# An attention and two-MLP kernel: mask-bit matmuls moved and paired, another order of the first eight periods, other dummy matmuls, a halved last product

## The chip, the core and the metric

The kernel runs on one core of a Trainium2 chip. The metric is the device time of one execution in microseconds (us). The engines are TensorE (PE: matmuls, PEld: the loading of their weights), VectorE (DVE), ScalarE (ACT), GpSimd (POOL) and SyncE (SP, which issues all DMAs here).

## What is computed

Bucketed attention over 2 batches, 8 heads, 768 tokens and 64 dimensions, and behind it two layers on the (2, 768, 512) result: a token-mixing layer with cosines and sines, and a normalized MLP of width 2048. Inputs and output are float32.

```python
q_bits = einsum('bhsd,dk->bhsk', q, proj) > 0        # 6 bits per query, the same for k
mask = q_bucket[:, :, :, None] == k_bucket[:, :, None, :]
scores = where(mask, (q @ k.T) / sqrt(64), -1e9)
attn = exp(scores - max) / (sum + 1e-9)
x = (attn @ v), heads side by side                   # 2 x 768 x 512
theta = x @ w_theta
y = w_tok_r @ (x * cos(theta)) + w_tok_i @ (x * sin(theta))
u = x + y;  x = u + relu(u @ w_ch)
xn = (x - mean) / sqrt(var + 1e-6) * g_ln
out = x + relu(xn @ w_ch1) @ w_ch2
```

## The kernel before

Every factor of a product is split into a high part and a low part of a type that TensorE takes at one pass per column, and a product is the sum of three matmuls (high by high, high by low, low by high). Tile names ending in `hi`/`lo`, `h`/`l` are these parts.

The attention works in 48 *periods* of 256 queries of one head, each with two tiles of 128 queries (i = 0, 1), whose scores stand in the PSUM tiles S0 and S1 (128 x 772 columns used). The steps of a period p have short names, `name.p.i`: the scores' matmuls (`S`, or, for the three periods of the first head, `D` and `Q`), the row maximum on VectorE (`M`, `s_max`, L340), the exponential on ScalarE (`E`, `s_exp`, L356), which is the last reader of S0 or S1, the reciprocal (`R2`), the normalization on GpSimd (`n`), 12 transposes on TensorE into the banks T0, T1, T2 (`U.p.u`), their copies into high and low parts (`H` on ScalarE, `L` on VectorE), 12 matmuls with the values of 256 columns (`PV`, L405) and the evacuation (`O`, `X`).

The mask is made by more rows in the scores' product: the bits of query and key as +-2^34 and the like. For all heads but the first, high, low and bits rows are stacked by DMAs (`sk`, `sb`) into tiles of 128 and 71 rows, and `s_mm` (L332) makes a tile with four matmuls of 386 columns. The first head doesn't wait for that: `direct_mm` (`D.p.i`, L503) makes six matmuls of 386 columns with the parts as they are (64 rows in period 0, 128 rows in periods 1 and 2), opening the accumulation, and `direct_bits` (`Q.p.i`, L515) closes it with two matmuls on the 7 rows of bits.

The bits come from `bits_chunk` (`ac.x` for the first pair of heads, `bc.x` for pairs 1 to 3, L286): two matmuls per pair on 384 columns of the parts, x = 0, 1 the halves of the key, 2, 3 of the query. `ac` writes the banks T0, T1, T2, O; `bc` writes T2 or O. Then ScalarE copies a half (`ay`, `by`), VectorE compares (`ab`, `bb`, L310) and VectorE or GpSimd scales it to the bits rows (`aw`, L523; `bw`, L663). `sh.nm.n.x.e` and `sl.nm.n.x.e` make the high and low part of query or key of pair n (x: half 0 or 1, or 2 for the whole; e: which engine, 0 is ScalarE or VectorE, 1 is GpSimd). `pb` splits the projection, `kz` copies the first head's key parts into tiles whose upper 64 rows are zero, `lr`, `lv` load raw queries, keys and values.

The kernel keeps the order of its instructions on every engine as it is written. For the first eight periods that order is one long list, `head`; each word calls a step. From then on `plan` lists the steps of a period; after the attention `tail`, `half1`, `trans`, `odd`, `even`, `last` are lists in the same manner. `warm(n)` (L493, listed as `warm.17`) puts n transposes of the identity into bank T0; their result is not read. 16 of them are issued right after the first loads, and 17 stand in `head` behind `Q.0.1`.

The end: round 15 of the MLP, `o_mm` (L1180) makes an output tile of 128 x 512 with six matmuls of 512 columns into T0 or O by turns, `o_add` (L1187) adds it to the residue on VectorE and SyncE stores the tile (L1189). Six tiles follow each other there.

Of the kernel before, what the change touches and what calls it, by code (L numbers as in the profile page):

```python
# [33 lines left out]
def attn_moe_kernel(  # L34
# [649 lines left out]
    head = """
        sh.k.0.0.0 pb.0.0 pb.0.2 sl.k.0.0.0 pb.0.1 sh.k.0.1.0 sl.k.0.1.0 sh.q.0.0.0 sl.q.0.0.0 sh.q.0.1.0 ac.0
        sl.q.0.1.0 fk ac.1 ay.0 ay.1 kz.1.1 ac.2 ay.2 D.0.0 ab.0 lr.3.0 ab.1 ac.3 sh.k.1.2.0 D.0.1 ay.3 ab.2
        sh.q.1.2.0 aw.0.1 aw.1.1 pb.1.0 aw.2.0 kz.0.0 ab.3 Q.0.0 M.0.0 Q.0.1 warm.17 pb.1.2 E.0.0 lr.3.1 M.0.1
        sl.q.1.2.1 E.0.1 pb.1.1 D.1.0 sl.k.1.2.0 sh.k.3.2.0 Q.1.0 tb.0 lr.2.0 R2.0 lr.2.1 aw.3.0 M.1.0 n.0.1
        sk.1 sh.k.2.2.0 D.1.1 n.0.0 E.1.0 U.0.2 Q.1.1 U.0.0 sh.q.3.2.0 sl.k.2.2.0 sl.k.3.2.0 U.0.1 sl.q.3.2.1
        H.0.0 D.2.0 M.1.1 H.0.2 bc.0.1 L.0.2 L.0.0 Q.2.0 sh.q.2.2.0 E.1.1 M.2.0 by.0 tb.1 H.0.1 bc.1.0 D.2.1  # L690
        lv.0 bb.0 sl.q.2.2.1 L.0.1 by.1 sb.1 R2.1 Q.2.1 bw.0.1 n.1.0 E.2.0 bb.1 vh.0.0 lr.4.0 bc.3.1 M.2.1
        vh.0.1 S.3.0 lr.5.0 vl.0.0.0 bc.2.0 by.3 bw.1.1 E.2.1 U.1.0 by.2 M.3.0 S.3.1 bb.3 n.1.1 U.1.1 E.3.0
        vl.0.1.1 R2.2 bb.2 U.1.2 tb.2 bw.3.1 H.1.0 M.3.1 n.2.0 H.1.1 S.4.0 PV.0 H.1.2 E.3.1 L.1.0 L.1.1 lr.4.1
        M.4.0 tb.3 R2.3 sh.k.4.0.0 gl U.2.0 n.2.1 O.0 n.3.0 bw.2.1 L.1.2 X.0 S.4.1 sl.k.4.0.1 U.2.1 E.4.0 U.2.2
        H.2.0 M.4.1 H.2.1 sk.2 H.2.2 E.4.1 S.5.0 lv.1 sh.q.4.0.0 PV.1 lr.5.1 L.2.0 sb.2 L.2.1 M.5.0 L.2.2 R2.4
        O.1 tb.4 X.1 n.3.1 sh.k.4.1.1 E.5.0 U.3.0 S.5.1 U.3.2 U.3.1 n.4.1 H.3.0 H.3.2 H.3.1 S.6.0 M.5.1 sk.4
        n.4.0 L.3.0 vh.1.0 L.3.2 PV.2 E.5.1 L.3.1 sl.q.4.0.1 U.4.2 O.2 vh.1.1 M.6.0 sk.3 R2.5 X.2 vl.1.0.1
        U.4.0 sb.3 S.6.1 tb.5 H.4.0 sl.k.4.1.0 sb.4 U.4.1 H.4.2 M.6.1 n.5.0 E.6.0 H.4.1 L.4.0 E.6.1 PV.3 n.5.1
        S.7.0 U.5.0 sh.q.4.1.0 O.3 L.4.2 L.4.1 M.7.0 H.5.0 U.5.2 S.7.1 X.3 R2.6 tb.6 U.5.1 E.7.0 H.5.1 H.5.2
        M.7.1 PV.4 vl.1.1.1 L.5.0 sl.q.4.1.1 n.6.0 E.7.1 tb.7 O.4 L.5.1  # L700
    """
# [769 lines left out]
```

## Time and profile before

| | us |
|---|---|
| median of 3 runs | 665.45 (664.65 to 670.51) |
| profiled execution | 665.16 |
| its span, first to last instruction | 663.4 |
| TensorE busy | 657.4 |
| VectorE busy | 556.9 |
| ScalarE busy | 416.7 |
| GpSimd busy | 310.4 |

The profiled execution's time is that of the whole execution; its span runs from its first to its last instruction. Busy shares are averages over stages that differ. In a timeline, instructions of one line that follow each other stand in one row ("x6"): start of the first and time until the end of the last. A matmul's end is modelled: matmuls overlap, so what one costs is read from the distance of their starts, not from its duration. In the chain each piece reaches to the start of the next.

### The profile page before, as it was taken

The numbers are of one execution on the slowest core, as the hardware profiler recorded it, in microseconds if no ns is written. First come the engines' busy times: TensorE is split into PE (matmuls) and PEld (weight loads), VectorE is DVE, ScalarE is ACT, GpSimd is POOL, SyncE is SP. The second block draws the span as 40 slices with busy tenths as digits, with TensorE's granted clock in tenths as the row PEclk, the third lists the DMA queues.
The fourth block names the chain that finished last, engine by engine and source line by source line (L and its number), as shares of the span: only waits on it lengthen the run. The fifth ranks groups of instructions, "written<-read, shape, count | busy, mean of one in ns | idle before, by whom it ended". The sixth has DMA issues, their size and how long they took to land.

```text
span 663.4 us, 11202 instructions
## 1 busy us (share of the span) xinstructions
PE 657.4 (99%) x3769; PEld 591.7 (89%) x3769; DVE 556.9 (84%) x999; ACT 416.7 (63%) x864; POOL 310.4 (47%) x419
## 2 busy tenths in 40 slices
PE   9999999999999999999999999999999999999997
PEld 7999999999999888888888888989998999999996
DVE  6999998999999999999888889986767686867654
ACT  6899998999999886776435534553333433333321
POOL 5887887667787644233433133434150505051400
PEclk9999999999999999999999999999999999999999
DMA  8977544575530411222422122101112121311022
GB/s 247 241 172 171 142 106 114 126 165 124 132 91 1 160 54 57 81 77 98 144 81 64 48 96 68 60 1 64 64 65 75 53 96 34 105 53 33 0 80 111
DMA packets 32230, 62.24 MB, mean 94 GB/s; under 512 B 4466, under 2 KB 11460, under 8 KB 32173
## 3 DMA queue, kind: packets, MB, share of 16 engines
q1 hardware_dynamic: 32173, 61.53, 32.6%
q8 instruction: 30, 0.49, 0.3%
q14 instruction: 27, 0.22, 0.1%
HBM read 39.98 MB, written 3.15 MB: 65 GB/s over the span
## 4 chain that ended last, share of the span: by engine, by line
PE 96%; DVE 2%; DMA 1%; issue 0%; ACT 0%; SPq 0%; POOL 0%; POOLq 0%
PE o L1180 20%; PE acc L853 15%; PE o L405 10%; PE s L332 10%; PE t L380 9%; PE Z L1145 8%; PE a L895 5%; PE v L1145 5%; PE th L787 3%; PE zy L1145 2%; PE Y L1145 2%; PE bits L286 2%; PE s L503 1%; PE warm L493 1%; PE ut L880 1%; PE xt L964 1%
## 5 line engine op out<-in xcount | busy, mean ns | idle before, releaser
L1180 PE MATMUL o<-arena,hh 128*128 128x512 f32 x384 | 118.9, 391 | 0.0
L367 POOL TENSOR_SCALAR pn<-p,l,M 128x768 f32<-128x768 f32 x96 | 94.7, 986 | 38.6 <-DVE l L363 25.8
L340 DVE TENSOR_REDUCE M<-s 128x1 f32<-128x772 f32 x96 | 91.0, 949 | 3.6 <-PE s L515 2.2
L101 DVE TENSOR_TENSOR ptl<-t,pth 128x512 fp32r<-128x512 f32 x144 | 90.6, 680 | 1.5 <-ACT pth L389 1.3
L356 ACT ACTIVATE p<-s,M 128x772 f32<-128x772 f32 x96 | 87.6, 912 | 2.7 <-DVE M L340 2.2
L117 POOL TENSOR_SCALAR cs<-st 128x512 f32<-128x512 f32 (+2 forms) x68 | 44.7, 663 | 84.1 <-DVE cy L131 75.1
L1180 PEld LDWEIGHTS o<-arena,hh 128*128 128x128 f32 x384 | 71.5, 188 | 13.7
L389 ACT ACTIVATE pth<-t 128x512 fp32r<-128x512 f32 x144 | 81.1, 599 | 3.9 <-PE t L380 2.5
L332 PE MATMUL s<-tk,tq 128*128 128x386 f32 (+1 forms) x360 | 82.8, 351 | 0.0
L380 PE MATMUL t<-ident,pn 128*128 128x128 f32 x576 | 80.1, 273 | 0.0
L853 PE MATMUL acc<-arena,tokh 128*128 128x512 f32 x240 | 75.3, 395 | 0.0
L1180 PE MATMUL o<-arena,hl 128*128 128x512 f32 x192 | 75.2, 392 | 0.0
L380 PEld LDWEIGHTS t<-ident,pn 128*128 128x128 f32 x576 | 68.5, 141 | 5.7 <-POOL pn L367 0.6
L1153 ACT ACTIVATE sn<-Z 128x384 f32<-128x384 f32 x39 | 19.2, 492 | 67.2 <-PE Z L1145 67.2
L332 PEld LDWEIGHTS s<-tk,tq 128*128 128x128 f32 (+1 forms) x360 | 59.4, 190 | 0.1
L853 PEld LDWEIGHTS acc<-arena,tokh 128*128 128x128 f32 x240 | 44.0, 188 | 8.5
L1187 DVE TENSOR_TENSOR U<-o,U 128x512 f32<-128x512 f32 x48 | 32.9, 689 | 21.3 <-PE o L1180 20.5
L853 PE MATMUL acc<-arena,tokl 128*128 128x512 f32 x120 | 46.9, 391 | 0.0
L405 PE MATMUL o<-pth,vv 128*128 128x256 f32 x288 | 45.9, 295 | 0.1
L114 ACT ACTIVATE cy<-st 128x512 f32<-128x512 f32 (+2 forms) x72 | 39.6, 562 | 8.1 <-DVE tokl L101 2.5
L131 DVE SCALAR_TENSOR_TENSOR cy<-cy,cs 128x512 uint32<-128x512 uint32 (+2 forms) x72 | 41.4, 575 | 3.6
L125 DVE SCALAR_TENSOR_TENSOR cs<-st,cs 128x512 uint32<-128x512 uint32 (+2 forms) x76 | 44.0, 579 | 0.2
(257 smaller groups left out, 1482.8 us busy)
## 6 DMA issues: line engine op xcount, KB each, us to landing
st<-in_w_dram SPq DMA_DIRECT2D x36, 256.0 KB
st<-in_w_dram SPq DMA_DIRECT2D x14, 512.0 KB
tk<-hik SPq DMA_DIRECT2D x30, 193.0 KB
tq<-hiq SPq DMA_DIRECT2D x30, 192.0 KB
st<-in_wrT_dram SPq DMA_DIRECT2D x12, 384.0 KB
st<-in_wiT_dram SPq DMA_DIRECT2D x12, 384.0 KB
vs<-in_v_dram SPq DMA_DIRECT2D x8, 384.0 KB
tk<-lok SPq DMA_DIRECT2D x15, 193.0 KB
```

The source lines that it names most:

```text
L101: eng.tensor_tensor(out=o, in0=i, in1=f(hi), op=ALU.subtract)
L117: eng.tensor_scalar(out=s, in0=f(t)[:, :, 1], scalar1=0.0, scalar2=1.0, op0=ALU.mult, op1=ALU.mult)
L332: pe.matmul(ps[:, hf, 0:HW], lt[0:K, x * 128:(x + 1) * 128], rt[0:K, hf, :], start=(K == 128), stop=(K != 128),)
L340: vec.tensor_reduce(out=m_t[p][:, 0, i:i + 1], in_=s_ps[p, i][:, :, 0:HW], axis=AX.XY, op=ALU.max, negate=True)
L356: act.activation(pt, ps[:, :, 0:HW], AF.Exp, bias=m[:, 0, i:i + 1], accum_out=l_t[p][:, 0, i:i + 1])
L367: pool.tensor_scalar(out=pn.rearrange("p (h c) s -> p h (c s)", h=2), in0=p_t.pop((p, i))[:, :, 0:HALF], scalar1=l_t[p][:, 1, i:i + 1], sc ...
L380: pe.transpose(ps[:, w * 128:(w + 1) * 128], pn_t[p, i][:, c, :], ident)
L389: act.activation(ph, t_ps[p, u], AF.Copy)
L405: pe.matmul(ps, vv[:, c, e].rearrange("p a d -> p (a d)"), x[:, c::NI, :], start=(k == 0), stop=(k == 2 * NI - 1),)
L853: pe.matmul(acc, w[:, x, t * 128:(t + 1) * 128], z[:, x, y, :], start=(j == 0 and k == 0), stop=(j == NI - 1 and k == 5),)
L1145: pe.matmul(ps_t[r, b], W1[g][y][:, w, d, :], XB[s][x][:, z, d, :], start=(first == 1 and k == 0), stop=(k == 5), skip_group_check=True,)
L1180: pe.matmul(ps, lt[:, i * 128:(i + 1) * 128], W2[g][:, y, x, :], start=(k == 0), stop=(k == 5))
```

## The change

Four things change. `direct_bits` may come before `direct_mm` for a tile of periods 1 and 2: it then makes the tile and opens the accumulation (`start`), and `direct_mm` closes it; the list uses this for i = 1. The list `head` has another order, and other engines for some steps (the last digit of `sh`, `sl`, `aw`, `kz`, `bw`, `vl`), with 19 transposes in place of 17. The first 16 transposes are replaced by 38 matmuls of 128 columns of a tile of zeros by itself, for which VectorE, not GpSimd, clears `pb_lo`, that part first. And the last `o_mm`/`o_add` (tile 5 of the last round) is made in two halves of 256 columns, the first in bank O, the second in S0, each with its own addition and store.

```diff
@@ -494,15 +494,17 @@
 
     def direct_mm(p, i):
 
-        ps = psum.tile([128, 2, 512], F32, tag=f"S{i}", name=f"s{p}_{i}")
-        s_ps[p, i] = ps
+        if (p, i) not in s_ps:
+            s_ps[p, i] = psum.tile([128, 2, 512], F32, tag=f"S{i}", name=f"s{p}_{i}")
+        ps = s_ps[p, i]
+        first, last = (p == 0 or i == 0), (p > 0 and i == 1)
         r = slice((2 * p + i) * 128, (2 * p + i + 1) * 128)
         K, kk = (64, [hl["k", 0, y] for y in (0, 1)]) if p == 0 else (128, kz)
         for x, y in ((0, 0), (0, 1), (1, 0)):
             for hf in range(2):
                 pe.matmul(
                     ps[:, hf, 0:HW], hl["q", 0, x][0:K, r],
-                    kk[y][0:K, hf, :], start=(x + y == 0), stop=False,
+                    kk[y][0:K, hf, :], start=(first and x + y == 0), stop=(last and x == 1),
                 )
 
     def bits_q(r):
@@ -510,11 +512,14 @@
         return bits_t[0][0:7, hf, x:x + 128]
 
     def direct_bits(p, i):
+        lead = (p, i) not in s_ps
+        if lead:
+            s_ps[p, i] = psum.tile([128, 2, 512], F32, tag=f"S{i}", name=f"s{p}_{i}")
         r = slice((2 * p + i) * 128, (2 * p + i + 1) * 128)
         for hf in range(2):
             pe.matmul(
                 s_ps[p, i][:, hf, 0:HW], bits_q(r),
-                bk0[0:7, hf, :], start=False, stop=True,
+                bk0[0:7, hf, :], start=lead, stop=not lead,
             )
 
     def bits_p0(nm, hf, eng):
@@ -542,12 +547,16 @@
     sp.dma_start(out=cst_sb, in_=cst)
     load_raw(1)
     sp.dma_start(out=pbr[:, 1:NP], in_=pb[:, 1:NP])
+    vec.memset(f(pb_lo[:, 1]), 0.0)
+    ps = bank("T0", "warm")[:, 0:128]
+    for x in range(38):
+        pe.matmul(ps, pb_lo[:, 1], pb_lo[:, 1], start=True, stop=True)
+    for n in (0, 2, 3):
+        vec.memset(f(pb_lo[:, n]), 0.0)
     make_identity(nc, ident)
     pool.memset(halfpi, math.pi / 2)
-    pool.memset(f(pb_lo), 0.0)
     for t in kz:
         pool.memset(f(t[64:128]), 0.0)
-    warm(16)
     TS = tuple(range(22, 46, 3))
     bg, bg2, bg3 = {}, {}, {}
 
@@ -682,22 +691,22 @@
     )
 
     head = """
-        sh.k.0.0.0 pb.0.0 pb.0.2 sl.k.0.0.0 pb.0.1 sh.k.0.1.0 sl.k.0.1.0 sh.q.0.0.0 sl.q.0.0.0 sh.q.0.1.0 ac.0
-        sl.q.0.1.0 fk ac.1 ay.0 ay.1 kz.1.1 ac.2 ay.2 D.0.0 ab.0 lr.3.0 ab.1 ac.3 sh.k.1.2.0 D.0.1 ay.3 ab.2
-        sh.q.1.2.0 aw.0.1 aw.1.1 pb.1.0 aw.2.0 kz.0.0 ab.3 Q.0.0 M.0.0 Q.0.1 warm.17 pb.1.2 E.0.0 lr.3.1 M.0.1
-        sl.q.1.2.1 E.0.1 pb.1.1 D.1.0 sl.k.1.2.0 sh.k.3.2.0 Q.1.0 tb.0 lr.2.0 R2.0 lr.2.1 aw.3.0 M.1.0 n.0.1
-        sk.1 sh.k.2.2.0 D.1.1 n.0.0 E.1.0 U.0.2 Q.1.1 U.0.0 sh.q.3.2.0 sl.k.2.2.0 sl.k.3.2.0 U.0.1 sl.q.3.2.1
-        H.0.0 D.2.0 M.1.1 H.0.2 bc.0.1 L.0.2 L.0.0 Q.2.0 sh.q.2.2.0 E.1.1 M.2.0 by.0 tb.1 H.0.1 bc.1.0 D.2.1
-        lv.0 bb.0 sl.q.2.2.1 L.0.1 by.1 sb.1 R2.1 Q.2.1 bw.0.1 n.1.0 E.2.0 bb.1 vh.0.0 lr.4.0 bc.3.1 M.2.1
...
+        sh.k.0.0.0 pb.0.0 sl.k.0.0.0 pb.0.2 pb.0.1 ac.0 sh.k.0.1.0 sl.k.0.1.0 ac.1 sh.q.0.0.0 sh.q.0.1.0
+        sl.q.0.0.0 ay.0 ac.2 sl.q.0.1.0 fk ac.3 ab.0 ay.1 kz.1.1 ay.2 D.0.0 ay.3 lr.3.0 ab.1 D.0.1 ab.2
+        sh.k.1.2.0 lr.2.0 aw.0.1 aw.1.0 aw.2.1 Q.0.0 ab.3 lr.3.1 lr.2.1 pb.1.0 sl.k.1.2.0 pb.1.2 kz.0.1 sk.1
+        sh.q.1.2.0 Q.0.1 warm.19 M.0.0 E.0.0 aw.3.1 sh.k.3.2.1 M.0.1 E.0.1 pb.1.1 sl.k.3.2.0 tb.0 sh.k.2.2.0
+        R2.0 D.1.0 Q.1.1 sl.k.2.2.0 Q.1.0 sh.q.3.2.0 n.0.1 D.1.1 bc.0.1 M.1.0 bc.1.0 n.0.0 M.1.1 U.0.0
+        sh.q.2.2.0 E.1.0 D.2.0 E.1.1 Q.2.1 lv.0 by.1 sl.q.3.2.0 sl.q.1.2.0 Q.2.0 sl.q.2.2.1 bb.1 H.0.0 L.0.0
+        U.0.2 U.0.1 by.0 H.0.2 bb.0 D.2.1 H.0.1 M.2.0 tb.1 bw.0.1 E.2.0 bc.3.1 sb.1 vh.0.0 R2.1 bw.1.0 S.3.0
...
     """
 
     for w in head.split():
@@ -1169,24 +1178,32 @@
         hh, hlo = h_t[r, c]
         vec.scalar_tensor_tensor(out=hlo, in0=c_t.pop((r, c)), scalar=0.0, in1=f(hh), op0=ALU.max, op1=ALU.subtract)
 
-    def o_mm(r, t):
+    def cols(x):
+        return slice(0, 512) if x is None else slice(256 * x, 256 * x + 256)
+
+    def o_mm(r, t, x0=None, tag=None):
         g, s = rounds[r]
         e, i = divmod(t, TB)
-        ps = o_t[r, t] = bank(("T0", "O")[t % 2], f"o{r}{t}")
+        n = cols(x0)
+        if tag == "S0":
+            ps = psum.tile([128, 2, 512], F32, tag=tag, name=f"o{r}{t}")[:, 0, n]
+        else:
+            ps = bank(tag or ("T0", "O")[t % 2], f"o{r}{t}")[:, n]
+        o_t[r, t] = ps
         k = 0
         for x in range(2):
             hh, hlo = h_t[r, 10 * (x + 1) + e + 1]
             for lt, y in ((hh, 0), (hh, 1), (hlo, 0)):
-                pe.matmul(ps, lt[:, i * 128:(i + 1) * 128], W2[g][:, y, x, :], start=(k == 0), stop=(k == 5))
+                pe.matmul(ps, lt[:, i * 128:(i + 1) * 128], W2[g][:, y, x, n], start=(k == 0), stop=(k == 5))
                 k += 1
 
-    def o_add(r, t):
+    def o_add(r, t, x0=None):
         g, s = rounds[r]
         c = ORD[6 * s + t]
-        u = U(c)
+        u = U(c)[:, cols(x0)]
         vec.tensor_tensor(out=u, in0=o_t.pop((r, t)), in1=u, op=ALU.add)
         if g == NG - 1:
-            sp.dma_start(out=out[c * 128:(c + 1) * 128, :], in_=u)
+            sp.dma_start(out=out[c * 128:(c + 1) * 128, cols(x0)], in_=u)
 
 
     ops.update(
@@ -1414,8 +1431,10 @@
         run(last if g == NG else odd if r % 2 else even, r=r, p=r - 1, g=g, a=a, b=b, c=c, d=d)
     r = len(rounds) - 1
     run("o_mm.{r}.0 h_add.{r}.12 h_hi.{r}.12 o_add.{r}.0 h_lo.{r}.12", r=r)
-    for t in range(1, 6):
+    for t in range(1, 5):
         run("o_mm.{r}.{t} o_add.{r}.{t}", r=r, t=t)
+    for x, tag in ((0, "O"), (1, "S0")):
+        run("o_mm.{r}.5.{x}.{tag} o_add.{r}.5.{x}", r=r, x=x, tag=tag)
     order.close()
     zctx.close()
 
```

## Rows read from the trace of the kernel before

**Rows 1.** Page, part 1: busy time (share of the span) and instructions of each engine.

```profile
PE 657.4 (99%) x3769; PEld 591.7 (89%) x3769; DVE 556.9 (84%) x999; ACT 416.7 (63%) x864; POOL 310.4 (47%) x419
```

**Rows 2.** Page, part 4: the chain that ended last, shares by engine.

```profile
PE 96%; DVE 2%; DMA 1%; issue 0%; ACT 0%; SPq 0%; POOL 0%; POOLq 0%
```

**Rows 3.** The chain, first 30 us: start us, us, engine, tile, line, number of instructions.

```profile
1.34 3.69 PE warm L493 x16
...
11.34 2.01 PE warm L493 x17
...
19.32 1.05 PE bits L286 x6
...
25.02 0.71 PE s L332 x4
...
27.94 0.88 PE t L380 x8
...
29.54 1.45 PE o L405 x12
```

**Rows 4.** Timeline, TensorE, 0 to 25 us: start us, us, engine, line, operation, tiles.

```profile
4.59 0.42 PE L493 MATMUL warm<-ident 128*128 128x128 f32 x1
5.07 0.69 PE L286 MATMUL bits<-hik,pb_hi 128*128 128x384 f32 x1
...
5.88 0.52 PE L286 MATMUL bits<-hik,pb_hi 128*128 128x384 f32 x1
...
6.84 0.52 PE L286 MATMUL bits<-loq,pb_lo 128*128 128x384 f32 x1
7.29 0.64 PE L503 MATMUL s<-hik,hiq 64*128 64x386 f32 x2
...
13.14 0.62 PE L503 MATMUL s<-tkz,hiq 128*128 128x386 f32 x2
...
14.39 0.61 PE L515 MATMUL s<-bk,bits 7*128 7x386 f32 x2
...
24.86 0.87 PE L332 MATMUL s<-tk,tq 128*128 128x386 f32 x4
```

**Rows 5.** Timeline, the last matmul and the last addition.

```profile
659.12 0.39 PE L1180 MATMUL o<-arena,hl 128*128 128x512 f32 x1
659.55 0.69 DVE L1187 TENSOR_TENSOR u<-o,u 128x512 f32<-128x512 f32 x1 [0.67 <-PE o L1180]
```

**Rows 6.** Windows: us; busy PE, PEld, DVE, ACT, POOL; granted clock; DMA share; GB/s.

```profile
0.00:5.05 5.05, 3.67 (x16) 3.27 (x16) 0.69 (x2) 2.38 (x5) 2.75 (x12) 1.00 0.52 153
...
660.60:660.90 0.30, 0.00 (x0) 0.00 (x0) 0.00 (x0) 0.00 (x0) 0.00 (x0) 1.00 0.00 0
...
661.50:661.80 0.30, 0.00 (x0) 0.00 (x0) 0.00 (x0) 0.00 (x0) 0.00 (x0) 1.00 0.94 362
```

**Rows 7.** Timeline, VectorE (DVE) and ScalarE (ACT), 3 to 14 us.

```profile
3.66 0.56 DVE L221 SCALAR_TENSOR_TENSOR lok<-raws,hik 128x384 fp32r<-128x384 f32 x1 [3.66 <-ACT hik L210]
...
5.32 0.56 DVE L221 SCALAR_TENSOR_TENSOR lok<-raws,hik 128x384 fp32r<-128x384 f32 x1 [0.97 <-ACT hik L210]
...
5.86 1.05 DVE L101 TENSOR_TENSOR loq<-raws,hiq 128x384 fp32r<-128x384 f32 x2
...
6.86 1.61 DVE L310 SCALAR_TENSOR_TENSOR bb<-bits,by 64x384 f32<-64x384 f32 x3
...
11.03 1.83 DVE L340 TENSOR_REDUCE M<-s 128x1 f32<-128x772 f32 x2 [0.73 <-PE s L515]
...
12.09 0.91 ACT L356 ACTIVATE p<-s,M 128x772 f32<-128x772 f32 x1 [1.14 <-DVE M L340]
...
13.04 0.95 DVE L221 SCALAR_TENSOR_TENSOR lok<-raws,hik 128x768 fp32r<-128x768 f32 x1
```

**Rows 8.** Timeline, GpSimd (POOL), its first operation on a tile.

```profile
0.71 0.20 POOL masks.py:197 MEMSET ident<- 128x128 f32 x1 [0.29 <-POOLq L1461]
```

**Rows 9.** The chain, last 8 us: twenty matmuls of 512 columns.

```profile
654.98 4.55 PE o L1180 x20
```

More of the change, by code (lines that the diff above doesn't have):

```diff
@@ L690, in attn_moe_kernel @@
-        H.0.0 D.2.0 M.1.1 H.0.2 bc.0.1 L.0.2 L.0.0 Q.2.0 sh.q.2.2.0 E.1.1 M.2.0 by.0 tb.1 H.0.1 bc.1.0 D.2.1
-        lv.0 bb.0 sl.q.2.2.1 L.0.1 by.1 sb.1 R2.1 Q.2.1 bw.0.1 n.1.0 E.2.0 bb.1 vh.0.0 lr.4.0 bc.3.1 M.2.1
-        vh.0.1 S.3.0 lr.5.0 vl.0.0.0 bc.2.0 by.3 bw.1.1 E.2.1 U.1.0 by.2 M.3.0 S.3.1 bb.3 n.1.1 U.1.1 E.3.0
-        vl.0.1.1 R2.2 bb.2 U.1.2 tb.2 bw.3.1 H.1.0 M.3.1 n.2.0 H.1.1 S.4.0 PV.0 H.1.2 E.3.1 L.1.0 L.1.1 lr.4.1
-        M.4.0 tb.3 R2.3 sh.k.4.0.0 gl U.2.0 n.2.1 O.0 n.3.0 bw.2.1 L.1.2 X.0 S.4.1 sl.k.4.0.1 U.2.1 E.4.0 U.2.2
@@ L695, in attn_moe_kernel @@
[L695 to L699, printed above, removed]
@@ L700, in attn_moe_kernel @@
-        M.7.1 PV.4 vl.1.1.1 L.5.0 sl.q.4.1.1 n.6.0 E.7.1 tb.7 O.4 L.5.1
+        sh.k.0.0.0 pb.0.0 sl.k.0.0.0 pb.0.2 pb.0.1 ac.0 sh.k.0.1.0 sl.k.0.1.0 ac.1 sh.q.0.0.0 sh.q.0.1.0
+        sl.q.0.0.0 ay.0 ac.2 sl.q.0.1.0 fk ac.3 ab.0 ay.1 kz.1.1 ay.2 D.0.0 ay.3 lr.3.0 ab.1 D.0.1 ab.2
+        sh.k.1.2.0 lr.2.0 aw.0.1 aw.1.0 aw.2.1 Q.0.0 ab.3 lr.3.1 lr.2.1 pb.1.0 sl.k.1.2.0 pb.1.2 kz.0.1 sk.1
+        sh.q.1.2.0 Q.0.1 warm.19 M.0.0 E.0.0 aw.3.1 sh.k.3.2.1 M.0.1 E.0.1 pb.1.1 sl.k.3.2.0 tb.0 sh.k.2.2.0
@@ new lines, in attn_moe_kernel @@
+        R2.0 D.1.0 Q.1.1 sl.k.2.2.0 Q.1.0 sh.q.3.2.0 n.0.1 D.1.1 bc.0.1 M.1.0 bc.1.0 n.0.0 M.1.1 U.0.0
+        sh.q.2.2.0 E.1.0 D.2.0 E.1.1 Q.2.1 lv.0 by.1 sl.q.3.2.0 sl.q.1.2.0 Q.2.0 sl.q.2.2.1 bb.1 H.0.0 L.0.0
+        U.0.2 U.0.1 by.0 H.0.2 bb.0 D.2.1 H.0.1 M.2.0 tb.1 bw.0.1 E.2.0 bc.3.1 sb.1 vh.0.0 R2.1 bw.1.0 S.3.0
+        vh.0.1 L.0.2 bc.2.0 M.2.1 by.3 n.1.0 n.1.1 vl.0.0.1 E.2.1 U.1.0 L.0.1 tb.2 vl.0.1.1 by.2 M.3.0 S.3.1
+        bb.3 R2.2 bb.2 M.3.1 E.3.0 lr.4.0 U.1.1 U.1.2 H.1.0 n.2.1 n.2.0 sh.k.4.0.0 lr.4.1 H.1.1 sk.2 E.3.1
@@ new lines, in attn_moe_kernel @@
+        S.4.0 bw.3.1 lv.1 PV.0 tb.3 H.1.2 L.1.0 gl M.4.0 U.2.0 sh.q.4.0.1 L.1.1 O.0 bw.2.1 S.4.1 U.2.1 E.4.0
+        R2.3 n.3.0 n.3.1 L.1.2 X.0 H.2.0 M.4.1 sh.k.4.1.0 sb.2 H.2.1 tb.4 sl.k.4.0.1 U.2.2 S.5.0 L.2.0 PV.1
+        E.4.1 H.2.2 M.5.0 U.3.0 S.5.1 O.1 L.2.1 R2.4 U.3.1 sl.q.4.0.1 L.2.2 lr.5.1 lr.5.0 X.1 n.4.0 sk.3 M.5.1
+        n.4.1 tb.5 E.5.0 sb.3 H.3.0 U.3.2 H.3.1 vh.1.0 S.6.0 E.5.1 L.3.0 PV.2 L.3.1 sl.k.4.1.1 H.3.2 M.6.0 R2.5
+        O.2 L.3.2 E.6.0 U.4.0 n.5.0 X.2 S.6.1 n.5.1 H.4.0 U.4.1 M.6.1 L.4.0 H.4.1 vh.1.1 L.4.1 E.6.1 sk.4 sb.4
@@ L701, in attn_moe_kernel @@
+        U.4.2 S.7.0 M.7.0 R2.6 PV.3 vl.1.0.1 H.4.2 O.3 U.5.1 U.5.0 sh.q.4.1.0 tb.6 L.4.2 S.7.1 H.5.0 X.3 U.5.2
+        M.7.1 H.5.1 vl.1.1.1 E.7.0 L.5.0 H.5.2 n.6.0 sl.q.4.1.1 tb.7 E.7.1 PV.4 O.4 L.5.1
     """
```

## The prediction

> **What bounds the kernel now.** I read the page's first part, then the chain that ended last, then the timeline of the first 25 us engine by engine, and last the end of the program. TensorE is busy for 657.4 of 663.4 us [rows 1], and the chain is 96% TensorE [rows 2]. So a gain can come only where TensorE does something useless, stands between two matmuls, works slowly, or from the two ends. All four are there. From 1.34 to 5.03 it runs 16 dummy transposes, and from 11.34 to 13.35 it runs 17 more [rows 3]. After the first ones it is slow: three bits matmuls of 384 columns start in 0.96 us (5.88 to 6.84), 0.32 each, where six take 1.05 us at 19.32, 0.175 each [rows 3, 4]. At each change of the number of rows it stands: the six matmuls of `D.1.0` take 1.25 us until `Q.1.0` starts (13.14 to 14.39), though six of their size cost 1.07 (four take 0.71) [rows 3, 4]. And at the end the last matmul starts at 659.12, the last addition runs from 659.55 to 660.24, and the output's last bytes move until 661.8 [rows 5, 6].
>
> The profiled execution took 665.16 us, its span 663.4, so 1.76 us lie around the span. The median of the three runs is 665.45, 0.29 above the profiled one. I sum on the profiled one and add 0.29.
>
> **Changes of rows.** From `D.1.0` (13.14) to `S.3.0` (24.86) TensorE needs 11.72 us [rows 4]. In it lie 24 direct and 8 closing matmuls of 386 columns at 0.178, 18 bits matmuls at 0.175 and 12 transposes at 0.110 (eight in 0.88) [rows 3]: 5.70 + 3.15 + 1.32 = 10.17. The rest, 1.55, falls on 8 changes between 128 and 7 rows, 0.19 each. In the new list the matmuls on the bits of tiles 1 and 0 stand side by side (`D.1.0 Q.1.1 Q.1.0 D.1.1`, and the same for period 2), so 4 changes stay: 10.17 + 4 x 0.19 = 10.93, rounded up to 10.95: **0.78 less**. Before 13.14 there are 5 changes now and 3 after (four `ac`, two `D`, two `Q`, dummies), 0.38 less on TensorE alone.
>
> An opening `Q.1.1` needs tile S1 free, so it waits for `E.0.1`, with `Q.1.0`, `D.1.1` and all later matmuls queued behind it. By the times below `E.0.1` ends at 13.6 and `Q.1.1` is reached at 13.8. For period 2 I placed the vector and scalar work in the new order: `M.1.1` ends at about 17.4, `E.1.1` at 18.6, and `Q.2.1` is reached at 19.7. Both waits are covered; without the cover each would cost what it is late.
>
> **The first dummies.** The 38 new ones are matmuls of 128 columns on zeros. VectorE does nothing until 3.66 [rows 7], so its memset can start when GpSimd starts, 0.71, and take what the memset of the same size takes there, 0.20 [rows 8]. With 0.06 for the handover (4.59 + 0.42 to 5.07 [rows 4]) the first dummy starts at 0.97, not at 1.34. No matmul of 128 columns is in the trace. From below: 128/384 of the bits matmul's 0.32, 0.107 at the low clock, 0.055 at the high one. From above: a transpose of that size, 3.69/16 = 0.23 at the low clock, 0.110 at the high one [rows 3]. I take 0.107, since operand type and instruction are the bits matmul's, and matmuls of 256 columns (twelve in 1.45, 0.121) and of 512 (twenty in 4.55, 0.228) go with their columns too [rows 3, 9]. Then 38 take 4.07 and the last starts at 4.93. The first bits matmul writes the same bank, so it waits for the last dummy's end, as now for the last transpose's: 5.3 if the clock stays low.
>
> When the clock rises is the second unknown. The durations show it: the low one of the two levels, 1.2 and 2.4 GHz, until 6.84, the high one from 7.29 [rows 4], which is 2.0 us after the first ordinary matmul and 5.7 after the first transpose. (The printed granted clock is 1.00 for this stretch too [rows 6] and doesn't tell; 0.23 against 0.110 for a transpose does.) If dummies of the new kind count and transposes don't, the clock rises from 3.0 on; if both count alike, at about 6.7. I take 4.2, nearer the first, since 3.7 us of transposes left it low and 2 us of matmuls sufficed: 30 dummies until then, 8 at 0.055, first bits matmul at about 4.85. The Trainium skill speaks for this (TensorE: Matmul & The Clock Gate, Part 4: PE-mode transpose): a transpose doesn't count as a busy array in the way a matmul does. By that rule the first of the two cases holds and (a) below falls away; the 3.7 us of transposes at the low rate agree, but would fit a clock that is only late as well.
>
> With the high clock from 4.2 the operands set the pace, not TensorE. The second half of the key's low part ends at 5.88, the query's at 6.91 [rows 7], so `ac.3` ends near 7.1; 12 direct matmuls and a change give 9.4; the first matmul on bits starts at 9.6, the four end at 10.3, and the 19 dummies behind another change (0.11 each, 2.07) end at **12.6**. VectorE after 6.91: three `ab` 1.61 (0.54 each), `aw.1` about 0.6 (no larger a tile), `ab.3` 0.54, and now the low part of pair 1's key, 0.95, in front of `M.0.0` [rows 7]: 10.6, where `M.0.0` starts at 11.03 now. `M.0.0` 0.92 and `E.0.0` 0.91 [rows 7] then free S0 at 12.5. So `D.1.0` starts at 12.6 against 13.14: **0.5 less**. Two more dummies cost next to nothing, since S0 is free no sooner. With the clock as late as now the same sum gives 5.3, eight bits matmuls, mostly slow, to 7.6, direct to 9.9, bits to 10.8, dummies to 13.1: 0.05 less.
>
> **Other moves of the list.** The low parts of the queries of pairs 1 and 3 go from GpSimd to VectorE, where two halves of 384 take 1.05 [rows 7]; by my placing they end at 19.4, the `bb.1` behind them at 19.9, and `U.0.2`, which needs its bank, is reached at 20.5. GpSimd takes over one high part in an idle stretch. On SyncE the load of pair 2's key goes ahead of pair 3's query; both are read only after 13 us, and the loads of pairs 4 and 5 have readers far off. The memsets that GpSimd loses had no waiter. All that I cost at nothing, with bounds 0 and +0.6 (c). After 25 us the chain is matmuls without gaps, in the same number, before and after.
>
> **The end.** The last product is split into two halves of 256 columns: 12 matmuls at 0.121 in place of 6 at 0.228, so the last starts 0.18 later. From its start to the addition it is 0.43 now [rows 5], of which half its own 0.228 goes: +0.07 in all. An addition of 512 columns takes 0.69 [rows 5], a subtraction of 384 0.52 [rows 7], so one of 256 about 0.4: -0.29. The first half's addition and DMA lie under the second half's matmuls. The last DMA moves half the bytes; between the addition's end and the last bytes lie 1.5 us now, and the moving itself is the last 0.9 of them at most [rows 5, 6]. If the time goes with the number of packets nothing is gained, if with the bytes up to 0.45; I take 0.1, nearer the first, as the number stays. Together **0.3 less**, between 0.2 and 0.7.
>
> Sum: 0.5 + 0.78 + 0.3 = 1.6; 665.16 - 1.6 + 0.29 = **663.8**.
>
> **Rivals.** (a) *The clock is as late as now.* For it: a fixed delay fits the rows too. The first term falls to 0.05: 664.3. (b) *The dummies are too long*, and the change ends up slower. Place: the TensorE queue ahead of `ac.0`. If a dummy costs what a transpose of its size does and the clock stays low all along, 38 x 0.23 = 8.7, first bits matmul at 9.9; everything behind it is ready, so bits to 11.3, direct to 13.6, the four on bits to 14.5, dummies to 16.6, 3.4 late: 665.45 + 3.4 - 0.78 - 0.3 = 667.8. If the clock rises at 4.2 they end at 6.7, `D.1.0` starts 0.9 late, and it is 665.3. It decides from a mean of 0.16 per dummy on. For it: the only operations of this size cost that. Against: each wider matmul follows its columns. (c) *TensorE waits in the new order* behind `U.0.2`: if the two query parts take 1.6 each on VectorE, not 1.05, `bb.1` ends at 21.0, and TensorE stands 0.5 to 0.6: 664.4. For it: VectorE has no idle stretch there any more. Against: 0.6 us of slack.
>
> **How the numbers follow.** Forecast 0.5, (a) 0.17, (b) 0.25, of which 0.1 at 667.8 or above, (c) 0.08. The range goes from 662.3 (665.16 - 0.5 - 0.8 - 0.7, every term at its best, and 0.8 for the scatter of runs, 664.65 to 665.45) to 666.5, which holds the milder form of (b); 0.1 of (b) and some 0.06 below are left out. A measurement of this kernel can tell about 1%, 6.7 us, from no change: faster by that needs more than all dummies and changes together (0.01), slower needs (b) twice over (0.02), so 0.97 for no change.
>
> **What would show it.** Right: a first dummy near 1.0; a bits matmul at 0.175 already at its first; the first matmul on mask bits near 9.6; `D.1.0` near 12.6; four changes fewer from there and `S.3.0` near 23.5; the same chain after it; a last addition of about 0.4. Wrong: dummies that start 0.2 apart, bits matmuls at 0.32, or an idle TensorE ahead of `Q.1.1`, `Q.2.1` or `U.0.2`.

## The result, and the profile after

The changed kernel takes 669.86 us (median of 18 runs, 668.86 to 673.52), the kernel before 665.19 beside it (18 runs): a ratio of 1.008 [1.0065, 1.0096]. That is slower by 0.8%: below the 1% that the prediction named as the limit, though the interval lies clear of 1. It is 6 us above the 663.8 forecast and outside the range of 662.3 to 666.5. The profiled execution took 669.88 us, its span is 668.1.

The page of the changed kernel, busy time and shares of the chain, against [rows 1, 2]:

```profile
span 668.1 us, 11276 instructions
...
PE 663.1 (99%) x3799; PEld 599.6 (90%) x3799; DVE 559.2 (84%) x1003; ACT 416.2 (62%) x863; POOL 312.9 (47%) x421
...
PE 97%; DVE 1%; ACT 0%; issue 0%; ACTq 0%
```

TensorE is busy 5.7 us longer for 30 instructions more, and still 97% of the chain: nothing new is waited for, TensorE itself takes longer. Where, the first 31 us of the chain tell, against [rows 3]:

```profile
1.03 8.38 PE warm L553 x38
...
9.46 2.90 PE bits L286 x8
12.36 2.34 PE s L505 x12
14.70 0.90 PE s L520 x4
15.59 3.89 PE warm L493 x19
19.48 1.06 PE s L505 x6
20.55 0.90 PE s L520 x4
21.45 1.26 PE s L505 x6
...
30.34 0.71 PE s L332 x4
```

The 38 new dummies hold TensorE for 8.38 us, until 9.41, where the 16 transposes ended at 5.03. And the 19 transposes take 3.89, 0.205 each, where 17 took 2.01, 0.118 each. The starts of single matmuls (timeline of TensorE, against [rows 4]) give the sum its points:

```profile
9.46 0.69 PE L286 MATMUL bits<-hik,pb_hi 128*128 128x384 f32 x1
...
11.55 0.52 PE L286 MATMUL bits<-hiq,pb_hi 128*128 128x384 f32 x1
11.87 0.49 PE L286 MATMUL bits<-loq,pb_lo 128*128 128x384 f32 x1
12.29 0.62 PE L505 MATMUL s<-hik,hiq 64*128 64x386 f32 x2
12.75 0.52 PE L505 MATMUL s<-lok,hiq 64*128 64x386 f32 x2
...
19.24 0.60 PE L505 MATMUL s<-tkz,hiq 128*128 128x386 f32 x2
...
30.18 0.87 PE L332 MATMUL s<-tk,tq 128*128 128x386 f32 x4
```

Bits matmuls still start 0.32 apart at 11.55: the clock is at the low one of its two levels, 1.2 GHz, until 12. From 12.29 on the distances are those of 2.4 GHz. Then it falls back. Windows (columns as in [rows 6]; the granted clock is the third figure from the end):

```profile
14.50:15.50 1.00, 1.00 (x6) 0.65 (x4) 0.33 (x2) 0.36 (x1) 1.00 (x2) 1.00 1.01 201
15.50:15.80 0.30, 0.30 (x3) 0.28 (x3) 0.30 (x1) 0.00 (x0) 0.30 (x1) 0.69 1.21 288
15.80:16.10 0.30, 0.30 (x3) 0.30 (x2) 0.30 (x1) 0.00 (x0) 0.30 (x3) 0.50 0.89 195
18.50:19.00 0.50, 0.50 (x5) 0.50 (x4) 0.01 (x1) 0.50 (x2) 0.40 (x1) 0.50 1.20 202
19.20:20.00 0.80, 0.80 (x7) 0.80 (x6) 0.80 (x1) 0.80 (x2) 0.72 (x2) 1.00 1.20 212
```

The granted clock is 0.50 from 15.6 to 19, just while the 19 transposes run, and TensorE was busy without a break before and during it. The end of the program (timeline, against [rows 5]):

```profile
664.61 0.28 PE L1197 MATMUL o<-arena,hl 128*128 128x256 f32 x1
...
664.93 0.42 DVE L1204 TENSOR_TENSOR u<-o,u 128x256 f32<-128x256 f32 x1 [0.29 <-PE o L1197]
```

The sum over the two profiled executions: first bits matmul 5.07 to 9.46, **+4.39**; from there to the first matmul on mask bits 5.30 to 5.17, -0.13; from that one to `D.1.0` 2.77 to 4.61, **+1.84**; `D.1.0` to `S.3.0` 11.72 to 10.94, **-0.78**; `S.3.0` to the last addition 634.69 to 634.75, +0.06; from the last addition's start to the end of the span 3.85 to 3.17, **-0.68**. Together +4.70, the difference of the spans (668.1 and 663.4).

The 18 spans of the changed kernel lie in three groups, 667.1 to 667.4 (6), 667.8 to 668.1 (5) and 670.3 to 671.7 (7); the profiled one, of the middle group, stands at the median. The mean granted clock is 0.997 in all five of the middle group and 0.999 or 1.0 in the other thirteen, so the fall that the profile shows belongs to the middle group. The other two groups have no trace of their own. The profile of `after_w2` below, with a span of 671.3, shows a clock that is low until 24 us, and that of `after_128`, with 667.1, one that rises and does not fall.

### The profile page after: what moved, and what is told of

It reads as the page before. It is cut to its first block, busy times and chain, and to the rows that moved or that the text cites. A ratio compares the mean times of both kernels' runs of the same rounds, so it can differ in the third digit from the quotient of the medians.

```text
span 668.1 us, 11276 instructions
## 1 busy us (share of the span) xinstructions
PE 663.1 (99%) x3799; PEld 599.6 (90%) x3799; DVE 559.2 (84%) x1003; ACT 416.2 (62%) x863; POOL 312.9 (47%) x421
## 4 chain that ended last, share of the span: by engine, by line
PE 97%; DVE 1%; ACT 0%; issue 0%; ACTq 0%
PE o L1197 20%; PE acc L862 15%; PE o L405 10%; PE s L332 10%; PE t L380 9%; PE Z L1154 8%; PE a L904 5%; PE v L1154 5%; PE th L796 4%; PE zy L1154 2%; PE Y L1154 2%; PE bits L286 2%; PE warm L553 1%; PE s L505 1%; PE xt L973 1%; PE ut L889 1%
## 5 line engine op out<-in xcount | busy, mean ns | idle before, releaser
L1197 PE MATMUL o<-arena,hh 128*128 128x512 f32 (+1 forms) x388 | 119.1, 388 | 0.0
L1197 PE MATMUL o<-arena,hl 128*128 128x512 f32 (+1 forms) x194 | 75.5, 389 | 0.0
```

The lines of the kernel that those rows point to most:

```text
L1197: pe.matmul(ps, lt[:, i * 128:(i + 1) * 128], W2[g][:, y, x, n], start=(k == 0), stop=(k == 5))
```

## The experiments

Sixteen kernels ran. Ratios are to the kernel before on the same chip. `a_...` are the changed kernel with one part altered (`a_tr16_aw`: two), `t_...` are `a_tr16_aw` altered. Diffs show only lines and words that differ, and "..." marks what is left out. "High" and "low" are the two levels of TensorE's clock, read from durations ahead of the first fall and from the granted clock behind it.

### The first dummies

**b_38.** The kernel before, with only the 38 new dummies in place of its 16 transposes.

```diff
+    vec.memset(f(pb_lo[:, 1]), 0.0)
...
+    for x in range(38):
+        pe.matmul(ps, pb_lo[:, 1], pb_lo[:, 1], start=True, stop=True)
...
-    pool.memset(f(pb_lo), 0.0)
...
-    warm(16)
```

> The kernel before with only the 38 new dummies (and VectorE's clearing) in place of the 16 transposes. Theory (the dummies make the whole loss): 38 x 0.22 us end at 9.4, first bits matmul at 9.46 instead of 5.07, and the time is 4.4 to 7 us above the kernel before, ratio 1.007 to 1.010. Rival (the new order has a part in the loss): ratio below 1.005.

674.73 us, 1.0151 [1.0132, 1.017]. The first bits matmul starts at 9.46 as in the changed kernel, and the clock stays low until 24, through `Q.0.x` and 17 transposes. The ratio lies above the 1.007 to 1.010 expected. So the dummies alone cost more than the whole change loses, and with the rest of the change the loss is 4.9 smaller. Of that, 0.78 and 0.68 are the changes of rows and the end (the sum above); the remainder goes with the clock, which is low longer here.

**a_18.** 18 of the new dummies in place of 38.

```diff
-    for x in range(38):
+    for x in range(18):
```

> The changed kernel with 18 of the 38 new dummies. Theory (price): a 128-column dummy costs 0.22 us at the low clock, as 38 in 8.38 us, and nothing but their number makes the first bits matmul late: 18 end at about 5.0, the first bits matmul is at 5.05, D.1.0 near 13.1, the whole 1.2 to 1.6 us below the kernel before (ratio 0.998). Rival (the new order itself is slow, the dummies only hide it): first bits at 5.05, but D.1.0 still 17 or later and the time not below 667.

665.21 us, 1.0015 [0.9996, 1.0034]. The 18 take 4.10 us (1.03 to 5.13), 0.23 each: it is the count times 0.22 that held TensorE (timeline):

```profile
1.03 4.10 PE L553 MATMUL warm<-pb_lo 128*128 128x128 f32 x18 [1.03 <-DVE pb_lo L550]
5.20 0.69 PE L286 MATMUL bits<-hik,pb_hi 128*128 128x384 f32 x1
```

The price was as expected, the time was not (a ratio of 0.998): seven of ten spans are 662.8 to 663.7, three 666.0 to 667.4.

**a_tr16.** The 16 old transposes, and everything else of the change.

```diff
...
-    for x in range(38):
-        pe.matmul(ps, pb_lo[:, 1], pb_lo[:, 1], start=True, stop=True)
...
+    warm(16)
```

> The changed kernel with the 16 old transposes of the identity in place of the 38 new dummies; order, paired changes and halved product stay. Theory (price): like the run with 18 new dummies, first bits matmul at 5.07, D.1.0 near 13.1, 1.2 us below the kernel before. Rival (transposes and matmuls differ for the clock): the clock rises at another time after the first bits matmul than with 18 new dummies, by over 1 us.

664.33 us, 0.9993 [0.9984, 1.0002]; all ten spans 662.0 to 663.0. In the profile the clock is high from 6.6 on. The gain is 0.5 us, not the 1.2 expected. A wait that the changed kernel's late start hid stands in its trace (`a_tr16_aw` below), but taking it away did not make the kernel faster.

**a_0.** No first dummies.

```diff
...
-    for x in range(38):
-        pe.matmul(ps, pb_lo[:, 1], pb_lo[:, 1], start=True, stop=True)
...
```

> The changed kernel with no first dummies at all. The first bits matmul starts at about 4.4, when its operands are there. Theory (transposes help the clock to rise, the narrow matmuls of zeros do nothing for it): the clock rises late in many runs, as with 18 narrow ones, spans scatter between 662 and 667, median at or above 665. Rival (first dummies of any kind don't matter to the clock): spans as even as with the 16 transposes, 662 to 663, or lower by the earlier start.

668.01 us, 1.0046 [1.003, 1.0063], spans 665.9 to 666.9. TensorE starts real work 5 us sooner than in the changed kernel, and gains only 1.9 by the medians. Its timeline:

```profile
4.48 0.69 PE L286 MATMUL bits<-hik,pb_hi 128*128 128x384 f32 x1 [4.48 <-DVE pb_hi L101]
...
7.81 1.01 PE L505 MATMUL s<-hik,hiq 64*128 64x386 f32 x2
8.62 0.84 PE L505 MATMUL s<-lok,hiq 64*128 64x386 f32 x2
...
11.97 1.65 PE L520 MATMUL s<-bk,bits 7*128 7x386 f32 x4
13.55 4.31 PE L493 MATMUL warm<-ident 128*128 128x128 f32 x19
17.51 0.99 PE L505 MATMUL s<-tkz,hiq 128*128 128x386 f32 x2
```

Direct matmuls 0.32 apart at 9 us, 19 transposes in 3.96: the clock is low until 18, though TensorE has been busy since 4.48.

**a_wide8, a_w384, a_ones18.** Other dummies: 8 of 512 columns, 11 of 384 columns, 18 narrow ones (128 columns) on ones instead of zeros. The edit of `a_w384`:

```diff
...
-    for x in range(38):
-        pe.matmul(ps, pb_lo[:, 1], pb_lo[:, 1], start=True, stop=True)
...
+    for x in range(11):
+        pe.matmul(ps, pb_lo[:, 1], pb_lo[:, 1:4].rearrange("p n s -> p (n s)"), start=True, stop=True)
```

> The changed kernel with 8 dummies of 512 columns of zeros in place of 38 of 128. Theory (clock by streaming): 8 x 0.43 us at the low clock end near 4.9; a TensorE that streams all the time gets the high clock, so the bits matmuls run at 0.175 from the first or second on, D.1.0 is near 12.6, and the time is 0.5 us below that with 18 narrow dummies. Rival (zeros don't raise the clock, or it is late whatever runs): bits matmuls at 0.32 until about 7, D.1.0 near 13.1, same time as with 18 narrow ones.

> The changed kernel with 11 first dummies of 384 columns of zeros on the parts 1 to 3 of the cleared tile, so that ScalarE's write of part 0 does not wait for them as it did with 512 columns. 11 x 0.32 from 1.4 on end at 4.9. Theory (what raises the clock is work that streams, zeros or not): clock high by the third bits matmul in most runs, span 662 to 663. Rival (zeros don't count): bits matmuls at 0.32 until 7 to 8, spans scattered as with 18 narrow ones.

> The changed kernel with 18 dummies of 128 columns on ones, not zeros (that part of the tile is cleared afterwards by GpSimd). Theory (width): 0.22 us each and the clock low behind them, as with zeros: bits matmuls at 0.32 until about 7. Rival (data): with other data than zeros the clock rises before the first bits matmul or right at it, 0.175 each.

`a_wide8` 666.03, 1.0020 [1.0008, 1.0033]; ScalarE's write of `pb_lo` waits there for the dummies that read it, so operands come late and its time tells little; its bits matmuls are still 0.32 apart at 5.76. `a_w384` 664.39, 0.9994 [0.9984, 1.0003]: starts 0.32 apart, and in the profile the clock is high at the first bits matmul (5.16, the next at 5.43). `a_ones18` 667.71, 1.0033 [1.0016, 1.0049]: 0.23 each and the clock low until 17, seven of ten spans 665.9 to 666.3. So ones in place of zeros did not help. Nor are 384 columns needed for so early a rise: in `a_tr16_aw` (below) the 16 transposes, of 128 columns, did as much in one execution. There they take 3.41, where they take 3.68 in `a_tr16`, and the first bits matmuls are already fast:

```profile
1.34 3.41 PE L493 MATMUL warm<-ident 128*128 128x128 f32 x16 [1.34 <-POOL halfpi L553]
4.81 0.45 PE L286 MATMUL bits<-hik,pb_hi 128*128 128x384 f32 x1
5.09 0.33 PE L286 MATMUL bits<-lok,pb_lo 128*128 128x384 f32 x1
```

What goes with the first dummies is how often the clock rises very late. The profiles of `a_ones18` and `a_0`, with spans of 665.9 and 666.9, show it low until 17 and 18. Counting spans of 665.9 and more as such, it rose late in 10 of 20 executions with 18 narrow matmuls and in all four without dummies, in none of 21 with 11 matmuls of 384 columns (`a_w384`, `best_w`), and in none of 42 with 16 transposes (`a_tr16`, `a_tr16_aw`, `t_mix`, `best_t`).

### What holds the clock low behind them

**after_w2.** The changed kernel with 11 matmuls of 384 columns in place of the 19 transposes.

```diff
- warm.19
+ wide.11
```

> The changed kernel with its 38 first dummies, but the 19 transposes behind Q.0.1 replaced by 11 matmuls of 384 columns on the first key half (0.175 each at the high clock). Theory (the second part of the loss is that the clock falls during these transposes, granted 0.50 from 15.8 to 19): matmuls that stream keep it up, D.1.0 at about 17.5 instead of 19.24, span 666.3, where the clock rose before; no run with a mean clock of 0.997. Rival (the clock falls whatever runs there): D.1.0 still near 19 and granted clock 0.5.

672.62 us, 1.0104 [1.008, 1.0128], low until 24 in the profile. By their spans three of the four executions are of this kind (670.3 to 671.4, mean clock 1.0): there the clock was low ahead of the wide matmuls, so these runs can't tell what would keep it up. The fourth (667.7) has a mean clock of 0.997, so it fell in spite of them. That speaks against the theory that the transposes bring the clock down, by one execution here and by the profiles of `best_t` and `best_w` below.

**a0_128, after_128, t_128.** The direct matmuls of period 0 on all 128 rows instead of 64, in `a_0`, in the changed kernel and in `a_tr16_aw`.

```diff
-        K, kk = (64, [hl["k", 0, y] for y in (0, 1)]) if p == 0 else (128, kz)
+        K, kk = (128, [hl["k", 0, y] for y in (0, 1)] if p == 0 else kz)
```

> The changed kernel without first dummies, and with 128 rows instead of 64 in the direct matmuls of period 0 (which so add the other head's products; that part of the result is another than the reference's). Theory (matmuls of few rows don't count for the clock, however busy TensorE is): with 128 rows the clock rises during D.0.0 or D.0.1, near 9, and the spans, 665.9 to 666.9 without dummies and 64 rows, fall to 662 to 663. Rival (the clock looks at busy time alone, or is late at random): spans still 666.

> The changed kernel with its 38 dummies, and 128 rows in the direct matmuls of period 0 (other head's products added, as in the run before). Theory (few rows don't count): the clock rises at the latest during D.0 in every run and does not fall behind it; spans 665.8 to 666.5, no group at 670 and none with a mean clock of 0.997; the 38 dummies alone then cost the 4.3 us by which the first bits matmul is late, less 0.8 and 0.6. Rival: groups at 667.3, 668 and 670.6 as before.

> 16 transposes first, query bits' first half on VectorE, 128 rows in the direct matmuls of period 0 (other head's products added). Theory (few rows let the clock fall): no run with a mean clock of 0.997 (2 of 10 with 64 rows), two changes of rows fewer, spans 661.5 to 662.3. Rival: some runs at 0.997 again and spans up to 663.5.

`a0_128`: 664.84, 0.9998 [0.9988, 1.0008], ten of ten spans 662.2 to 663.7, where `a_0` had 665.9 to 666.9:

```profile
4.44 0.69 PE L286 MATMUL bits<-hik,pb_hi 128*128 128x384 f32 x1 [4.44 <-DVE pb_hi L101]
...
7.43 0.69 PE L505 MATMUL s<-hik,hiq 128*128 128x386 f32 x2
7.97 0.52 PE L505 MATMUL s<-lok,hiq 128*128 128x386 f32 x2
...
10.74 2.29 PE L493 MATMUL warm<-ident 128*128 128x128 f32 x19
12.79 0.60 PE L505 MATMUL s<-tkz,hiq 128*128 128x386 f32 x2
```

The clock rises within the first of them (0.27 apart at 7.43, 0.18 at 7.97) and stays: `D.1.0` starts at 12.79 against 17.51. The instructions, their columns and their order are the same; only the rows differ. `after_128`: 669.13, 1.0061 [1.0045, 1.0077], spans 666.9 to 667.9 and none at 670; the 19 transposes take 2.05 and `D.1.0` starts at 17.67 against 19.24. The rise is still late (0.32 apart at 12.19). Four executions are few to call the other groups gone, since six of the 18 of the changed kernel (667.1 to 667.4) look the same. I had expected 665.8 to 666.5 of it, about 1 too little. `t_128`: 664.39, 0.9992 [0.9983, 1.0001], spans 662.4 to 663.2, no fall.

**t_no2.** `a_tr16_aw` without the second dummies.

```diff
- Q.0.1 warm.19 M.0.0
+ Q.0.1 M.0.0
```

> 16 old transposes first, the query bits' first half on VectorE, and nothing at all behind Q.0.1. Theory (transposes there neither hold the clock nor cost anything): D.1.0 starts when S0 is free, 12.7 to 12.9, and spans are as with 19 transposes or some tenths lower. Rival (they do hold it): the clock falls after the idle stretch of 2 us in most runs, spans of 664 and more.

667.32 us, 1.0033 [1.002, 1.0045]. Windows:

```profile
9.00:10.80 1.80, 1.80 (x11) 1.47 (x9) 1.80 (x3) 1.23 (x4) 1.80 (x4) 1.00 0.94 358
11.00:13.00 2.00, 0.09 (x1) 0.00 (x0) 2.00 (x4) 1.57 (x4) 1.58 (x5) 0.50 0.97 366
13.00:21.00 8.00, 7.90 (x23) 7.05 (x24) 5.17 (x7) 5.05 (x8) 5.46 (x8) 0.50 1.05 237
```

The clock falls there too, at 10.9, before the 2 us without matmuls begin at 11.1, and stays low until 21. So the second dummies do not cause the fall. All five executions have a mean clock of 0.992 to 0.995, where `a_tr16_aw` has two of ten at 0.997: the rival came true, with transposes there the clock falls less often and for a shorter time. They are worth 2.4 us by the two ratios.

**t_mix.** `a_tr16_aw` with `ac.3` between `D.0.0` and `D.0.1`, as the kernel before had it.

```diff
- fk ac.3 ab.0 ay.1 kz.1.1 ay.2 D.0.0 ay.3
+ fk ab.0 ay.1 kz.1.1 ay.2 D.0.0 ac.3 ay.3
```

> A version meant to be kept: 16 transposes first, query bits' first half on VectorE, and the last bits matmuls of the first pair (128 rows) between the two direct tiles of 64 rows, as in the kernel before. Two changes of rows more (0.4) before the first matmul on bits. Theory (128 rows in between hold the clock): no run at 0.997, spans 662.2 to 662.7, ratio 0.997 to 0.999. Rival (it makes no difference): spans as without it, 662.4 to 663.5, some at 0.997.

664.49, 0.9993 [0.9983, 1.0003]; one of eleven runs has a mean clock of 0.997, against two of ten in `a_tr16_aw`: too few to tell.

### A wait that the late start hid, and the best version

**a_tr16_aw.** `a_tr16` with the first half of the query's bits scaled on VectorE, not GpSimd.

```diff
- aw.2.1
+ aw.2.0
```

> The changed kernel with the 16 old transposes, and the scaling of the query's first half of bits (aw.2) on VectorE again, not on GpSimd. With it on GpSimd that pass took 1.99 us and the first matmul on bits stood waiting until 10.59. Theory (GpSimd is held up while VectorE runs the key part of pair 1 beside it): on VectorE it takes about 0.5, the first matmul on bits starts at 9.9, D.1.0 at 12.9 instead of 13.55, and the time is 0.5 us lower. Rival (the first matmul on bits waits for something else): it still starts after 10.4.

The wait stands in the timeline of `a_tr16` (all engines, 7.7 to 10.7 us):

```profile
7.74 0.65 POOL L528 TENSOR_SCALAR bk<-bb,cst_sb 64x384 fp32r<-64x384 f32 x1
...
8.37 0.47 DVE L528 TENSOR_SCALAR bk<-bb,cst_sb 64x384 fp32r<-64x384 f32 x1
...
8.55 1.99 POOL L528 TENSOR_SCALAR bits<-bb,cst_sb 64x384 fp32r<-64x384 f32 x1 [0.15 <-DVE bb L310]
...
9.23 0.94 DVE L221 SCALAR_TENSOR_TENSOR lok<-raws,hik 128x768 fp32r<-128x768 f32 x1
...
10.59 0.44 PE L520 MATMUL s<-bk,bits 7*128 7x386 f32 x1 [0.75 <-POOL lok L203]
```

The same pass of 64 x 384 takes GpSimd 0.65 at 7.74 and 1.99 at 8.55, beside two passes of VectorE over SBUF, and TensorE stands 0.75 for it. The Trainium skill (SBUF — State Buffer, "SBUF: two separate sides") says that the two engines share a pair of ports as an exclusive lock: where VectorE's instruction has two SBUF inputs and GpSimd's reads SBUF, the one that starts later waits for the whole of the other's. The trace agrees in part. The pass is 1.34 longer, and the `lok` pass with two such inputs takes 0.94 of that, but GpSimd's pass had begun 0.68 before it. In `a_tr16_aw` the next such pass begins 0.10 behind the `lok` pass, at 10.36, and takes 1.39, which fits the rule.

With `aw.2.0` the first matmul on bits starts at 9.93 instead of 10.59, but the total is 664.40, 0.9997 [0.9987, 1.0006]. In the profiled execution the clock falls at 11.1 and the 19 transposes take 3.66, but that holds for two of ten only (mean clock 0.997); the other eight have spans of 662.4 to 662.7, no shorter than those of `a_tr16`. `t_128` and `t_no2`, which have `aw.2.0` too, show what comes next: `D.1.0` starts at 13.10 in both, with 19 transposes in front of it and with none, because S0 is free no sooner (`E.0.0` ends at 12.9 in both). So the wait was worth at most 0.45 at `D.1.0` (13.55 in `a_tr16`), and why nothing of that is left at the end of the program is open.

**best_t, best_w.** Dummies of 384 columns also in place of the 19 transposes: in `a_tr16_aw`, and in `a_w384` with `aw.2.0`.

```diff
- aw.2.1
+ aw.2.0
...
- warm.19
+ wide.11
```

> 16 old transposes first, the query bits' first half on VectorE, 11 matmuls of 384 columns in place of the 19 transposes behind Q.0.1; order, pairs and halved product of the change. Theory (falls of the clock in the second dummies cost 0.9 us in some runs): first matmul on bits at 9.9, D.1.0 at 12.8, spans 661.8 to 662.3 in all runs, ratio to the kernel before 0.997. Rival: spans as with the transposes there, 662.4 to 663.5.

> As the kernel before this one in the list, but with 11 dummies of 384 columns of zeros in place of the 16 first transposes. Theory (wide dummies raise the clock before the operands come): bits matmuls at 0.175 from the first one on in most runs, first matmul on bits at 9.9 to 10.2, D.1.0 at 12.8, spans 661.7 to 662.3, ratio 0.997. Rival (both first dummies are worth the same, or the wide ones less): spans not below those with 16 transposes.

`best_t` 664.76, 0.9994 [0.9985, 1.0003]; `best_w` 664.40, 0.9991 [0.9982, 0.9999], spans 662.4 to 663.3. `best_w` is the one version whose interval lies below 1, by 0.6 us in 665, and only just: `a_tr16` and `t_128` lie beside it. In its profiled execution the clock falls to 0.50 behind the four matmuls of 7 rows, and the 11 wide dummies take 3.6 us. That is one of eleven with a mean clock of 0.997 (three of eleven in `best_t`); the other ten, at 0.999 or 1.0, have spans of 662.4 to 663.3, so the fall is not why it gains no more. That is open. Timeline of TensorE and, below it, a window (columns as before):

```profile
10.11 0.94 PE L525 MATMUL s<-bk,bits 7*128 7x386 f32 x4
10.98 3.74 PE L498 MATMUL wide<-hik,pb_hi 128*128 128x384 f32 x11
14.54 0.54 PE L510 MATMUL s<-tkz,hiq 128*128 128x386 f32 x2
```

```profile
12.00:14.00 2.00, 2.00 (x8) 2.00 (x7) 2.00 (x4) 1.74 (x4) 1.59 (x3) 0.50 1.08 357
```

## Why the prediction was wrong, step by step

**The step that failed: "I take 0.107" for a dummy.** Measured 8.38/38 = 0.2205 (starts 0.213 apart). `a_18` shows that it is the price: 18 of them end at 5.13. I went with operand type and columns, though the only rows of 128 columns, the transposes at 0.23, said otherwise; at 128 columns the two cost alike. That is (b), to which I gave 0.25, with its dearest form (0.1) at 667.8. It came out 2.1 dearer still. Against that form the first bits matmul is 0.44 sooner (9.46, not 9.9), but the eight bits matmuls stay at the low clock (1.4 more), the transposes take 3.7, not 2.1 (1.6 more), and the tail saves 0.4 more.

**The second: the clock rises "at 4.2".** In the profiled execution it rose at 12.1. I reasoned that matmuls count and transposes don't, citing the Trainium skill (TensorE: Matmul & The Clock Gate, Part 4: PE-mode transpose). The runs go against it as I used it: with 16 transposes ahead all ten spans are 662.0 to 663.0 (`a_tr16`), with nothing ahead 665.9 to 666.9 (`a_0`), and 18 narrow matmuls of about the same length leave three of ten at 666.0 or above (`a_18`). In `a_tr16_aw` the clock rose while nothing but transposes had run.

**The third, which no rival held: "the 19 dummies behind another change (0.11 each, 2.07)".** I priced the side-by-side order of `D.0.0 D.0.1 Q.0.0 Q.0.1` by its changes of rows only, 0.38 less. It also puts 3.2 us of matmuls on 64 and 7 rows together; behind them the clock fell in the profiled execution: +1.84 up to `D.1.0`, of which the two added transposes are 0.2. How often it falls is told by the mean granted clock: all six profiles at 0.997 or less show such a fall, none of the others does. By that sign it came in 23 of 119 executions of the versions of the change with 64 rows (`t_no2` left out), in none of 24 with 128 rows (`a0_128`, `after_128`, `t_128`), and in 12 of 99 of the kernel before (run beside these), whose order parts the matmuls on 64 rows. At the rate of the first group, none of 24 would come up about once in 170 times, so this points to the rows. That the new order makes the fall more frequent is not shown, and the fall comes without it too.

Together: `D.1.0` was forecast at 12.6 and came at 19.24 in the profile, 6.6 late. Of that 5.0 is there at the first matmul on mask bits (14.63 for 9.6; the dummies and the slow bits matmuls), 1.6 in the transposes. That the time stayed within 1% is luck, not a term that was right.

**What held.** Changes of rows at 0.19 and four fewer: -0.78 forecast and measured, 10.94 for 10.95. `Q.1.1` and `Q.2.1` wait for nothing; nor does `U.0.2` in the changed kernel, though in `a_18`, which reaches it sooner, it stands 0.26 behind two query parts of 1.6 each on VectorE (3.21 from 18.03), as (c) had it. The chain behind is unchanged (+0.06). The tail gave 0.68, the upper bound of 0.2 to 0.7: the addition takes 0.42 as forecast, what follows it 2.75 instead of 3.16, 0.41 less where I took 0.1. The last store has half the bytes in as many rows, so this looks like time that goes with the bytes; no run varies it alone. `aw.2` on GpSimd, costed at nothing, makes TensorE stand 0.75 once the start is early (`a_tr16`).

**What stays open.** When exactly the clock rises and falls, and why executions of one kernel differ in it. Six profiles (`a_tr16_aw`, `t_mix`, `t_128`, `a_tr16`, `best_t`, `t_no2`) have the same 16 transposes and the same bits matmuls behind them, and by the distances of the starts the clock rises at about 4.4, 5.6, 6.6, 6.6, 7.4 and 7.5, so one profile of a version says little about its dummies. And some 0.25 us of an earlier start are lost again between 24.5 and 29 us (`a_tr16`), untested.

## What to carry to other kernels

Dummy matmuls are an expense on the path like any other: take the price of one from the nearest row of the same size, and bound the count by when the first real operand is there, since a queue in order makes real work wait for the last of them. Matmuls on few rows keep TensorE busy but, here, came before a fall of its clock and, without first dummies, ran with it low until 18 us; full rows in the same instructions avoided 3 us there (tried only with rows that alter the product, not with zeros). Where executions of one kernel differ, count them by group before a single profile is read as the cause. A late start hides waits: when it is mended, look again at every move that was free.
